# A gated linear recurrence with a feed-forward layer on one core: the fourth pair of chunks laid out one token per partition, the first states scaled straight from PSUM, and a new written order

## The chip, the cores and the metric

The kernel runs on 1 NeuronCore of one Trainium2 chip. The core has five engines with their own instruction queues: TensorE (PE, matrix products and turns), VectorE (DVE), ScalarE (ACT), GpSimd (POOL) and SyncE (SP, which here issues only DMA). The metric is the device time of one execution in microseconds (us), lower is better. Times come from three runs without a profile and from one execution with a profile.

## The reference

Inputs in float32: q, k, v, f_logit of shape (4 batches, 8 heads, 768 tokens, 48), w_in (384, 2048), w_out (2048, 384). A gated linear recurrence runs along the tokens for each batch and head, its output is laid out as 3072 rows of 384, and a feed-forward layer with SiLU follows:

```python
f = 1.0 / (1.0 + np.exp(-f_logit))
for t in range(S):
    state = f[:, :, t, :, None] * state + np.einsum('bhd,bhe->bhde', k[:, :, t], v[:, :, t])
    y[:, :, t] = np.einsum('bhd,bhde->bhe', q[:, :, t], state)
x = y.transpose(0, 2, 1, 3).reshape(B * S, H * D)
h = x @ w_in
g = h * (1.0 / (1.0 + np.exp(-h)))
out = g @ w_out
```

## The kernel before, in words

**Tiling.** The 768 tokens of a batch are cut into 6 chunks of 128. A chunk of one batch is a unit, and two units make one of 12 pairs (table `PAIRS`, line 19). In a pair of form 'T' both units are consecutive chunks of one batch, and a partition holds two consecutive tokens of all heads; a load then moves pieces of 2 x 48 floats, 384 bytes. In a pair of form 'N' a partition holds one token of each unit, and a piece is 48 floats, 192 bytes. Pairs 0 to 3 are T and take the chunks 0 and 1 of the batches 0 to 3; the pairs 4 to 11 are N and take the same chunk of two batches.

**Steps of a unit**, by the names of the written order, with the line of their code:
- `f`, `q`, `k`, `v`: loads, on SP's queue (239). `wi`, `wo`: the weights in 4 pieces each, on POOL's queue (216, 219).
- `E`, `L`: exponential and logarithm on ACT (246, 258, 261), which give the log of the gate; `cs`: its running sum over the chunk, a product with a triangle on TensorE (322, 326 for T; 329, 332 for N); `ia`, `a`, `al`: exponentials of that sum on ACT (334, 276, 336).
- `ki`, `qg`: k and q times these factors, on VectorE or POOL (339). `vb`: v as bfloat16 (187 or 185: the two lines of the copy helper).
- `tq`: turn of both by TensorE (346), and `qkc`: the copy out of PSUM; or `qkD`: the turn by one DMA on SP's queue (354). The pairs 0 to 3 and a few later units use `tq`.
- `sc`: scores (363 for T, 367 for N); `at`: masking on VectorE (371).
- `y`, `yi`: products with the values and with the state (283, 379, 383); `d`: the chunk's own addition to the state (295 for T, 400 for N); `sd`: its sum with the state before, or for a first chunk a plain copy (404, 187 or 185); `su`: that times `al`, two pieces of 48 partitions, which gives the next state (414, on POOL).
- `yc`: y as bfloat16; then `yT` and `xc`, turn on TensorE (391) and copy; or `yD`, turn by DMA (395). This gives xT of the pair.
- `mi.P.j`: two of the 16 column blocks of x @ w_in for the 256 tokens of pair P (269); the pairs 0 and 1 do it in two halves of 128 tokens. `si.P.j`: SiLU on ACT (274). `mo.P.i.n`: a quarter of the sum over the 16 blocks for the output of unit i (304). `oc`, `so`: copy out of PSUM and store.

**Order.** Every engine goes through its steps in the order in which they stand in the string `PLAN` (line 37); a word is the step, the engine (P TensorE, A ACT, V VectorE, G POOL, S SP) and the number of the buffer that the result takes. A step that waits holds back all that stands behind it on its engine, and this goes for SP's loads and turns too. `idle.512.n` are n products without use, of 512 columns, which fill time on TensorE. PSUM has 8 buffers (`pb`), q, k and v have 6 each, f has 4. ACT changes its table of functions where the order goes from exponentials to SiLU or back (475, 507).

`su` reads `sd` where the order has such a step, and otherwise `d` in PSUM (408); both ways were in the code already:

```python
if ("sd", P, i) in names:
    src = at("sd", P, i)
else:
    src = at("d", P, i)[:, 0:HD].rearrange("p (n w) -> p n w", w=2 * D)
```

Of the kernel before, what the change touches and what calls it, by code (L numbers as in the profile page):

```python
# [22 lines left out]
    ('T', (3, 0), (3, 1)),  # L23
# [14 lines left out]
f.0.0:S:0 f.0.1:S: f.2.0:S:1 f.1.0:S:2 q.0.0:S:0 E.0.0:A:0 E.0.1:A: k.0.0:S:0 L.0.0:A:0 L.0.1:A: idle.512.11::0 cs.0.1:P:0 E.2.0:A:1 k.1.0:S:1  # L38
cs.0.0:P:1 ia.0.1:A:0 v.0.0:S:0 E.1.0:A:0 ia.0.0:A:1 q.1.0:S:1 a.0.0:A:2 L.1.0:A:1 qg.0.0:G:0 L.2.0:A:2 f.3.0:S:3 idle.512.5::2 cs.1.1:P:2 ki.0.0:V:
al.0:A:0 a.0.1:A:3 ki.0.1:V:1 cs.1.0:P:3 ia.1.1:A:4 cs.2.0:P:4 k.2.0:S:2 qg.0.1:V: ia.1.0:A:2 tq.0.0:P:5 ki.1.1:V:2 a.1.0:A:1 cs.2.1:P:6 ki.1.0:V:3  # L40
a.1.1:A:0 q.2.0:S:2 tq.0.1:P:7 vb.0.0:A:0 vb.0.1:V:1 ia.2.1:A:3 qkc.0.1:V:0 d.0:P:1,0 qkc.0.0:A: qg.1.0:V: v.1.0:S:1 qg.1.1:V: sd.0.0:A:0
idle.512.3::3 sc.0.0:P:3,7 al.2:A:1 ia.2.0:A:4 su.0.0:G:0 sc.0.1:P:5,1 f.4.0:S:0 at.0.0.1:V:0 E.3.0:A:0 at.0.0.0:V: tq.1.0:P:7 al.1:A:2 a.2.0:A:2
wi.1:G: v.2.0:S:2 at.0.1.0:V:1 tq.1.1:P:2 L.3.0:A:0 qkc.1.1:V:1 qkc.1.0:A: ki.2.1:G:4 idle.512.1::3 cs.3.1:P:3 at.0.1.1:V: cs.3.0:P:4 a.3.1:A:1
ki.2.0:V:0 wi.0:G: sc.1.0:P:5,2 ia.3.1:A:0 at.1.0.0:V:2 y.0:P:7,1 a.2.1:A:3 qg.2.0:G: al.3:A:3 yc.0.0:A:0 at.1.0.1:V: q.3.0:S:3 sc.1.1:P:6,3
vb.1.1:A:2 yi.0.1:P: qg.2.1:G: at.1.1.1:V:3 yT.0.0:P:5 vb.1.0:A:3 tq.2.0:P:7 yc.0.1:A:1 at.1.1.0:V: d.1:P:2,3 a.3.0:A:4 wi.2:G: yT.0.1:P:1 sd.1.0:A:1
tq.2.1:P:6 xc.0.1:V:0 ia.3.0:A:2 xc.0.0:V: su.1.0:G:0 k.3.0:S:3 y.1:P:2,1 qkc.2.0:A:0 sd.0.1:V:0 mi.0.3.0:P:4 yc.1.0:V:2 mi.0.3.1:P: wi.3:G:
qkc.2.1:V: yi.1.1:P: mi.0.2.0:P:5 yc.1.1:A:0 yT.1.0:P:0 su.0.1:G:0 mi.0.2.1:P: xc.1.0:V:1 E.4.0:A:1 yT.1.1:P:7 xc.1.1:V: sc.2.1:P:2,6 sd.1.1:V:1
sc.2.0:P:1,0 L.4.0:A:1 mi.1.2.1:P:7 at.2.1.0:V:0 mi.1.3.1:P:3 mi.1.3.0:P: at.2.0.0:V:1 k.4.0:S:4 mi.1.1.0:P:2 at.2.1.1:V: mi.1.1.1:P: mi.1.2.0:P:
at.2.0.1:V: si.0.2:A:0 mi.0.1.0:P:1 mi.0.1.1:P: si.1.1:A:1 mi.1.0.0:P:6 si.1.2:A: mi.0.0.1:P:5 vb.2.1:G:4 mi.1.0.1:P: vb.2.0:A:5 wo.0:G: mi.0.0.0:P:
# [24 lines left out]
xc.5.1:A: ki.8.1:V:1 q.8.1:S: yc.6.1:A:0 cs.7.0:P:5 vb.8.0:V:4 a.8.0:A:4 mi.5.0:P:1 yc.6.0:V:2 a.7.0:A:1 yD.6.1:S:2 oc.4.0:V:3 al.8.0:A:5 cs.7.1:P:6
# [35 lines left out]
def kernel(  # L110
# [10 lines left out]
    nc = tc.nc  # L121
    B, H, S, D = q.shape
# [57 lines left out]
    at = lambda *key: where[key]  # L180
# [360 lines left out]
```

## Time and profile before

| | us |
|---|---|
| Median of three runs (lowest to highest) | 186.18 (183.22 to 188.34) |
| The profiled execution | 181.74 |
| Its span, first to last instruction | 179.9 |
| TensorE busy in the span | 170.3 (95%) |
| ACT, VectorE, POOL busy | 134.9, 83.2, 59.9 |
| Packets of SP's DMA queue | 69.1% of 16 engines' span |
| Packets of POOL's DMA queue | 16.0% |

The span lies 1.84 us under the profiled execution's time; the profiled execution is 1.48 us under the lowest of the three runs and 4.44 us under their median. Each answer of the trace gives start and length in us from the span's first instruction. "L304" is line 304 of the kernel. In the view of stretches, each line has the stretch, its length, the busy time of PE, PE's weight loads, DVE, ACT and POOL, then the granted TensorE clock (1.00 is full), the DMA share and GB/s. In the view of waits a line is: who waited for whom, us in total, times, the longest. Steps in the text are named as in the written order, for example `y.7.1` for unit 1 of pair 7.

### The profile page before, as it was taken

What the parts mean: (1) busy time and instruction counts of PE and PEld (TensorE: products, weight loads), DVE (VectorE), ACT (ScalarE), POOL (GpSimd) and SP (SyncE); (2) the same over time, 40 slices, a digit from 0 to 9 for tenths busy, and PEclk for the clock granted to TensorE, in tenths of its full rate; (3) what the DMA queues carried; (4) which work ended last, traced back from release to release, by engine and by line L of the source; (5) the groups of instructions that cost most, each with busy time, mean ns of one, the idle gap of its engine ahead of it and who ended that gap; (6) DMA issues with size and microseconds to landing.
All of it is one profiled execution on the core that took longest, in us unless ns stands there. A gap on an engine that the chain in (4) does not pass through costs nothing.

```text
span 179.9 us, 4982 instructions
## 1 busy us (share of the span) xinstructions
PE 170.3 (95%) x2039; PEld 130.0 (72%) x2040; DVE 83.2 (46%) x165; ACT 134.9 (75%) x252; POOL 59.9 (33%) x107
## 2 busy tenths in 40 slices
PE   6978599999999999999999999998999999999992
PEld 2355589998666787679688877787866877887782
DVE  7089977343710263793666064551058758000010
ACT  4899759999936899887997969783896971278321
POOL 6027753695200370140464500581305220003030
PEclk9999879999999999999999999999999999999999
DMA  5999999999989997999949999698985951314043
GB/s 142 315 321 309 202 242 256 230 209 193 180 176 182 203 201 134 210 204 207 158 106 221 178 202 205 125 218 170 216 156 122 213 127 26 109 26 131 0 154 112
DMA packets 109574, 31.91 MB, mean 177 GB/s; under 512 B 103536, under 2 KB 109088, under 8 KB 109552
## 3 DMA queue, kind: packets, MB, share of 16 engines
q1 hardware_dynamic: 104928, 26.19, 69.1%
q0 software_dynamic: 4624, 5.41, 16.0%
q8 instruction: 16, 0.26, 0.6%
q14 instruction: 6, 0.05, 0.1%
HBM read 25.17 MB, written 4.72 MB: 166 GB/s over the span
## 4 chain that ended last, share of the span: by engine, by line
PE 84%; ACT 6%; DVE 3%; DMA 2%; issue 2%; POOL 0%; POOLq 0%; DVEq 0%
PE pb L304 33%; PE pb L269 33%; PE pb L459 3%; DMA xT<-yb 2%; ACT x L334 2%; PE pb L346 2%; PE pb L379 2%; PE pb L383 2%; PE pb L367 2%; DVE atm L371 2%; PE pb L329 2%; DVE qk L339 1%; PE pb L391 1%; PE pb L295 1%; PE pb L363 1%
## 5 line engine op out<-in xcount | busy, mean ns | idle before, releaser
L304 PE MATMUL pb<-w_out_sb,hT 128*128 128x384 bf16 (+1 forms) x416 | 70.7, 313 | 0.1
L269 PE MATMUL pb<-xT,w_in_sb 128*128 128x256 bf16 (+1 forms) x672 | 70.1, 257 | 0.7 <-DMA xT<-yb 0.5
L274 ACT ACTIVATE hT<-pb 128x512 bf16<-128x512 f32 x96 | 51.0, 611 | 23.2 <-PE pb L269 23.1
L269 PEld LDWEIGHTS <-w_in_sb 128*128 128x128 bf16 x672 | 56.9, 98 | 8.2 <-issue 0.9
L304 PEld LDWEIGHTS <-hT 128*128 128x128 bf16 x416 | 37.9, 97 | 18.1
L414 POOL TENSOR_TENSOR st<-sd,al 48x192 bf16<-48x192 f32 x40 | 20.6, 516 | 54.7 <-PE pb L379 18.2
L371 DVE TENSOR_TENSOR atm<-pb,triu 128x512 bf16<-128x512 f32 x32 | 20.0, 682 | 15.2 <-PE pb L367 15.2
L187 DVE COPY ob<-pb 128x384 f32<-128x384 f32 (+1 forms) x16 | 8.3, 526 | 36.0 <-PE pb L304 35.9
L334 ACT ACTIVATE x<-pb 128x384 f32<-128x384 f32 x48 | 22.0, 511 | 3.3 <-PE pb L329 1.5
L507 ACT ACT_TABLE_LOAD x17 | 21.8, 1283 | 0.3
L339 POOL TENSOR_TENSOR qk<-k,x 128x384 bf16<-128x384 f32 x11 | 11.4, 1038 | 14.9 <-DVE vb L187 13.5
L339 DVE TENSOR_TENSOR qk<-k,x 128x384 bf16<-128x384 f32 x13 | 11.9, 936 | 8.3 <-DMA k<-in_k_dram 5.4
L404 DVE TENSOR_TENSOR sd<-pb,st 128x384 f32<-128x384 f32 x16 | 8.6, 550 | 12.6 <-PE pb L400 6.1
L316 POOL DMA_DIRECT2D out_dram<-ob x7 | 4.0, 569 | 29.5 <-ACT ob L185 21.1
L339 DVE TENSOR_TENSOR qk<-q,x 128x384 bf16<-128x384 f32 x17 | 11.4, 688 | 3.3 <-DMA q<-in_q_dram 1.8
L246 ACT ACTIVATE e<-f 128x768 f32<-128x768 f32 (+1 forms) x13 | 10.5, 804 | 2.0 <-DMA f<-in_f_logit_dram 2.0
L185 ACT CAST yb<-pb 128x384 bf16<-128x384 f32 x16 | 7.6, 490 | 3.6 <-PE pb L383 2.4
L371 DVE TENSOR_TENSOR atm<-pb,mask 128x512 bf16<-128x512 f32 x16 | 10.1, 680 | 0.4 <-PE pb L363 0.4
L339 POOL TENSOR_TENSOR qk<-q,x 128x384 bf16<-128x384 f32 x7 | 7.1, 1019 | 7.4 <-ACT x L334 5.8
L459 PE MATMUL pb<-zero,triu 128*128 128x512 bf16 x19 | 7.1, 525 | 1.5 <-POOL triu masks.py:66 1.4
L185 ACT COPY ob<-pb 128x384 f32<-128x384 f32 (+1 forms) x10 | 4.4, 456 | 4.6 <-PE pb L304 4.6
L346 PE MATMUL pb<-ident,qk 128*128 128x128 bf16 x80 | 6.7, 234 | 0.4 <-DVE atm L371 0.4
(72 smaller groups left out, 153.2 us busy)
## 6 DMA issues: line engine op xcount, KB each, us to landing
f<-in_f_logit_dram SPq DMA_DIRECT2D x11, 384.0 KB, 5.5
k<-in_k_dram SPq DMA_DIRECT2D x16, 192.0 KB, 3.7
v<-in_v_dram SPq DMA_DIRECT2D x16, 192.0 KB, 4.3
q<-in_q_dram SPq DMA_DIRECT2D x16, 192.0 KB, 4.2
q<-in_q_dram SPq DMA_DIRECT2D x4, 384.0 KB, 5.2
k<-in_k_dram SPq DMA_DIRECT2D x4, 384.0 KB, 4.9
v<-in_v_dram SPq DMA_DIRECT2D x4, 384.0 KB, 7.3
w_in_sb<-in_moe_w_in_dram POOLq DMA_DIRECT2D x4, 384.0 KB, 7.5
```

Of the source, the lines that this page charges most:

```text
L185: nc.scalar.copy(dst, src)
L246: return nc.scalar.activation(e, at("f", P)[:, j * w:(j + 1) * w], AF.Exp, scale=-1.0)
L269: nc.tensor.matmul(h[:, i, cols], w_in_sb[:, kk, n * 128:(n + 1) * 128], at("xT", P)[:, kk, cols], start=(kk == 0), stop=(kk == KT - 1))
L274: return nc.scalar.activation(at("hT", P)[:, 2 * j:2 * j + 2, :], at("h", P, j).rearrange("p (n c) -> p n c", n=2), AF.Silu)
L304: nc.tensor.matmul(at("o", P, i)[:, cols], at("hT", P)[:, n, i * C:(i + 1) * C], w_out_sb[:, n, cols], start=(n == 0), stop=(n == NT - 1))
L334: nc.scalar.activation(at(kind, P, i).rearrange("p h d -> p (h d)"), at("cs", P, i)[:, 0:HD], AF.Exp, scale=1.0 if kind == "ia" else -1.0)
L339: ENG[eng].tensor_mul(at("qk", P, i)[:, j, :, 0:D], heads("qk"[j], P, i), at("ia" if j else "a", P, i))
L346: nc.tensor.transpose(t_ps[:, j, p, :], at("qk", P, i)[:, j, 2 * p:2 * p + 2, :], ident)
L371: ENG[eng].tensor_mul(at("atm", P, i)[:, r], at(f"s{r}", P, i).rearrange("p (n c) -> p n c", c=C), mask[:, None, :].to_broadcast([C, NP, C]))
L414: ENG[eng].tensor_mul(at("st", P, i)[lo:lo + D, :, r * D:(r + 1) * D], src[lo:lo + D, :, r * D:(r + 1) * D], al_of(P, i)[lo:lo + D, :, Non ...
L459: nc.tensor.matmul(buf["pb", int(got)][:, 0:rest[0]], triu, zero[:, 0:rest[0]], start=True, stop=True, skip_group_check=True)
L507: nc.scalar.preload_act_table_set(TABLES[mode])
```

## The change

Three things change.

1. Pair 3 is of form N instead of T: its two units are still the chunks 0 and 1 of batch 3, but a partition holds one token of each. Its loads have 192-byte pieces and are cut in two, each half the chunk of one unit. Since the load's address used to assume that the units of an N pair differ in the batch, one line is added that takes batch and chunk of the half's own unit. Pair 3's q and k are turned by TensorE (`tq.3.0`, `tq.3.1`), as before.
2. The steps `sd.0.0`, `sd.1.0`, `sd.2.0` and `sd.3.0` are gone from the order: `su` of these first chunks reads the products `d` in PSUM and runs on VectorE instead of POOL.
3. The whole written order is another one, with other engines and buffers for many steps. The dummy products are 27 instead of 20, in 6 places instead of 4.

A form of `qkD` for T pairs is added to the code and not used by the order.

```diff
@@ PAIRS
     ('T', (2, 0), (2, 1)),
-    ('T', (3, 0), (3, 1)),
+    ('N', (3, 0), (3, 1)),
     ('N', (0, 2), (1, 2)),
@@ PLAN, the beginning
-f.0.0:S:0 f.0.1:S: f.2.0:S:1 f.1.0:S:2 q.0.0:S:0 E.0.0:A:0 E.0.1:A: k.0.0:S:0 L.0.0:A:0 L.0.1:A: idle.512.11::0 cs.0.1:P:0 E.2.0:A:1 k.1.0:S:1
+f.0.1:S:0 f.0.0:S: f.3.0:S:1 q.0.0:S:0 f.1.0:S:2 E.0.1:A:0 k.0.0:S:0 E.0.0:A: L.0.1:A:0 L.0.0:A: v.0.0:S:0 idle.512.10::0 cs.0.0:P:0 cs.0.1:P:1
+a.0.0:A:0 k.1.0:S:1 ia.0.0:A:1 E.3.0:A:1 a.0.1:A:2 q.1.0:S:1 al.0:A:0 E.1.0:A:0 qg.0.1:V:0 qg.0.0:V:1 ia.0.1:A:3 f.2.0:S:3 ki.0.0:G: L.1.0:A:1
+ki.0.1:V: idle.512.6::2 cs.1.1:P:2 vb.0.1:A:0 f.3.1:S: vb.0.0:V:1 L.3.0:A:2 tq.0.1:P:3 ia.1.1:A:4 cs.1.0:P:4 v.1.0:S:1 ki.1.1:G:2 tq.0.0:P:5 a.1.0:A:2
+a.1.1:A:0 d.0:P:6,7 ia.1.0:A:1 qg.1.1:V: k.2.0:S:2 su.0.0:V:0 qg.1.0:G:3 idle.512.3::0 tq.1.1:P:0 q.2.0:S:2 qkc.0.1:V:0 E.2.0:A:0 cs.3.0:P:1 wi.0:G:
+sd.0.1:V:0 qkc.1.1:A:1 v.2.0:S:2 qkc.0.0:V: wi.1:G: L.2.0:A:0 idle.512.5::4 sc.0.0:P:4,6 ki.1.0:V: q.5.0:S:3 at.0.0.0:V:0 vb.1.1:G:2 idle.512.1::3
+tq.1.0:P:3 vb.1.0:G:3 at.0.0.1:V: qkc.1.0:A: sc.0.1:P:7,5 at.0.1.0:V:1 cs.2.1:P:0 al.3.0:A:1 cs.2.0:P:4 k.6.1:S:3 at.0.1.1:V: al.1:A:2 ia.2.1:A:3
...
@@ PLAN, around f.7.0 and the xT of pair 4
+mo.2.0.3:P: si.3.3:A: si.3.4:A: sc.4.1:P:3,5 sc.4.0:P:1,7 oc.1.0:A:4 at.4.1.0:V:0 v.7.1:S:4 d.5.1:P:6 d.5.0:P:4 mi.3.2:P:2 at.4.1.1:V: qkD.5.0:S:0
+sd.5.0:V:0 d.4.0:P:3 si.3.2:A: mo.3.0.0:P:5 qg.5.1:V: y.4.1:P:4 at.4.0.0:V:1 mo.3.0.1:P: yc.4.1:A:0 su.4.1:G:0 at.4.0.1:V: mo.3.1.0:P:2 oc.2.0:V:5
+cs.6.0:P:1 ki.6.1:V: qkD.5.1:S:1 mo.3.0.2:P: E.7.0:A:0 sd.4.0:V:1 y.4.0:P:4 mo.3.1.1:P: L.7.0:A:1 vb.7.1:V:5 q.7.0:S:1 su.4.0:G:0 yT.4.1:P:7
+mo.3.1.2:P: xc.4.1:A:0 v.6.1:S: yc.4.0:A:1 cs.7.0:P:0 sd.5.1:V:1 cs.7.1:P:3 yT.4.0:P:7 q.7.1:S: ia.7.1:A:1 mo.3.1.3:P: al.7.0:A:4 a.7.0:A:2
+mo.3.0.3:P: xc.4.0:A: oc.3.1:V:2 qkD.6.1:S:2 ia.6.0:A:4 mi.4.7:P:4 oc.3.0:V:1 ia.7.0:A:0 ki.6.0:G:0 al.7.1:A:5 a.7.1:A:3 mi.4.3:P:6 ki.7.1:V:4
...
@@ emit, loads of an N pair
                 n = 2 // parts
                 w = n * HD
+                if n == 1:
+                    b, c = us[j][0] - j, us[j][1]
                 src = SRC[kind].rearrange("b h s d -> s (b h) d")[c * C:(c + 1) * C, (b + j * n) * H:(b + (j + 1) * n) * H]
@@ emit, qkD
-            nc.sync.dma_start_transpose(out=at("qkT", P, i).rearrange("p j n c -> p (j n) c"), in_=at("qk", P, i).rearrange("p j h d -> p (j h d)"))
+            if T:
+                dst = at("qkT", P).rearrange("p j n g s c -> p (j n) g s c")[:, :, :, i]
+            else:
+                dst = at("qkT", P, i).rearrange("p j n c -> p (j n) c")
+            nc.sync.dma_start_transpose(out=dst, in_=at("qk", P, i).rearrange("p j h d -> p (j h d)"))
```

125 lines of the change are left out of this document (58 added, 67 removed).

## The prediction

> **What bounds the kernel now.** The page's head, its busy shares and its DMA slices are read first. What matters is that TensorE is nearly full and that the 16 DMA engines are close to full for two thirds of the span.
>
> ```profile
> span 179.9 us, 4982 instructions
> PE 170.3 (95%) x2039; PEld 130.0 (72%) x2040; DVE 83.2 (46%) x165; ACT 134.9 (75%) x252; POOL 59.9 (33%) x107
> ...
> DMA  5999999999989997999949999698985951314043
> ```
>
> The first `mi` step (first product with w_in) starts at 25.17 us by the timeline of TensorE. The last `mo` ends at 176.77: there the chain that ended last goes over to ACT's copy of ob.
>
> ```profile
> 25.17 0.84 PE L269 MATMUL pb<-xT,w_in_sb 128*128 128x128 bf16 x12
> ```
>
> ```profile
> 176.77 0.32 ACT ob L185
> ```
>
> The view of busy time by stretch, cut at these two points, shows where TensorE is empty.
>
> ```profile
> 0.00:25.17 25.17, 19.50 (x285) 12.33 (x287) 17.43 (x47) 19.55 (x41) 11.04 (x29) 0.93 1.06 259
> 25.17:176.77 151.60, 150.78 (x1760) 117.64 (x1754) 65.73 (x119) 115.09 (x212) 48.90 (x79) 1.00 0.84 166
> 176.77:179.90 3.13, 0.00 (x0) 0.00 (x0) 0.00 (x0) 0.31 (x1) 0.00 (x0) 1.00 0.26 84
> ```
>
> The middle stretch has 0.82 us of idle in 151.60. So nothing can be won there but work, and much can be lost: any wait that is put in front of TensorE lengthens the span one for one. The start (25.17 us) is where time can be won. The third view, the waits of TensorE, agrees: the only wait of more than 1.5 us is for the masking `at` on VectorE, in the start, and the only one for a transfer is 0.5 us.
>
> ```profile
> PE pb L391 <- DVE atm L371: 1.7, 1, 1.7
> PE pb L322 <- ACT lf L258: 1.5, 2, 1.2
> ...
> PE pb L269 <- DMA xT<-yb: 0.5, 1, 0.5
> ```
>
> So there are three sums: when the first `mi` starts, how much work stands behind it, and whether a load in the new order comes after TensorE wants it.
>
> **1. The start.** The first fence is VectorE's timeline, the second the timeline of all engines, the third the groups of instructions with shapes kept apart (busy us, mean ns).
>
> ```profile
> 11.04 0.56 DVE L339 TENSOR_TENSOR qk<-q,x 128x384 bf16<-128x384 f32 x1
> ...
> 12.73 0.68 DVE L187 COPY qkTT<-pb 128x1024 bf16<-128x1024 bf16 x1
> ...
> 17.86 3.02 DVE L339 TENSOR_TENSOR qk<-k,x 128x384 bf16<-128x384 f32 x1
> 20.80 2.47 DVE L371 TENSOR_TENSOR atm<-pb,mask 128x512 bf16<-128x512 f32 x4
> ...
> 24.70 0.55 DVE L404 TENSOR_TENSOR sd<-pb,st 128x384 f32<-128x384 f32 x1
> ```
>
> ```profile
> 18.48 1.97 POOL L339 TENSOR_TENSOR qk<-q,x 128x384 bf16<-128x384 f32 x2
> ```
>
> ```profile
> L414 POOL TENSOR_TENSOR st<-sd,al 48x192 bf16<-48x192 f32 x40 | 20.6, 516 | 54.7 <-PE pb L379 18.2 <-DVE sd L404 10.9 <-DVE qk L339 9.1
> ...
> L185 ACT COPY sd<-pb 128x384 f32<-128x384 f32 x3 | 1.5, 512 | 2.2 <-PE pb L295 2.2
> ...
> L187 DVE COPY ob<-pb 128x192 f32<-128x192 f32 x2 | 0.7, 358 | 21.4 <-PE pb L304 21.4
> ```
>
> Before, `ki.2.0` of the third pair stands on VectorE between the eight masking steps of pairs 0 and 1. It takes 3.02 us, all through the two POOL multiplications that run from 18.48 to 20.45, where the like step at 11.04 takes 0.56. The last mask ends at 20.80 + 2.47 = 23.27, `y.1` follows, and `mi` comes 1.9 us after that mask.
>
> After, VectorE's order from `qg.1.1` on is: `qg.1.1`, `su.0.0`, `qkc.0.1`, `sd.0.1`, `qkc.0.0`, `ki.1.0`, eight masks; nothing of pair 2 stands among them. `su.0.0` is new on VectorE: two pieces of 192 columns read from PSUM. No row shows this operation there; the nearest is the 192-column copy from PSUM at 358 ns, so 0.7 us (bounds: 0.4 us as it has 48 partitions and not 128, if that helped; 1.1 us if it went like the 550 ns of 384 columns). In exchange an ACT copy (0.51) and two POOL pieces (1.03) leave the way from `d.0` to the state, and the pairs 1 and 2 save the same; there VectorE has the cover of its 46%. At `su.3.0` the masks `at.3.1` stand behind it, and `y.3.1`, which waits for them, has some 2.6 us of other TensorE steps ahead; without that cover it would cost 0.7.
>
> The sum: 0.56 + 0.7 + 0.68 + 0.55 + 0.68 + 0.56 + 8 x 0.62 (2.47 / 4) = 8.7 us. It starts when q of pair 1 is in. DMA begins at about 2 us and goes at this rate (a GB/s line of the DMA view for 2 to 14 us):
>
> ```profile
> GB/s 183 262 266 274 280 169 230 306 320 323 302 323 325 324 324 324 326 301 291 306 323 317 305 321 325 324 327 325 326 321 325 323 328 316 310 306 328 320 301 303
> ```
>
> A 384 KB load (0.393 MB) at 320 GB/s is 1.23 us. Up to `q.1.0` the new order has seven of them and one half of `f.3` at 1.05 (worked out in part 3): 2.0 + 8.6 + 1.05 = 11.7, and some 0.5 to the waiting instruction, 12.2. The last mask ends at 20.9, and with the 1.9 us behind it the first `mi` would start at 22.8. To that I add 0.7 us for POOL: `ki.0.0`, `ki.1.1` and `qg.1.0` now run on POOL beside multiplications on VectorE. The bounds are 0 and three POOL pieces of 1.0 us each, 3.0; 0.7 is near the low end since only `qg.1.1` against `qg.1.0` falls on the chain. **First `mi` at 23.5, a gain of 1.7** (2.4 to -0.6).
>
> The Trainium skill, SBUF — State Buffer, section "SBUF: two separate sides", says that VectorE and GpSimd share a port pair under an exclusive lock, which a VectorE operation with two inputs in SBUF and a GpSimd operation hold for their whole length. The 3.02 us row agrees; taken for all three places it makes the upper bound of 3.0 and a rival below.
>
> The dummy products (`idle`) grow from 20 to 27. They stand in waits: `idle.512.6` ends near 9, and `cs.1.1` behind it waits for `L.1.0`, which ended at 10.5 before and has f of pair 1 about a microsecond later now; `idle.512.5` ends some 0.5 before `qkc.0.0`, by the VectorE sum. Without that cover each product costs about 0.22 (estimate: 512 columns by the 384-column products of part 2, 1.32 / 8).
>
> ```profile
> 8.98 1.58 ACT L258 ACTIVATE lf<-e 128x768 bf16<-128x768 f32 x2
> ```
>
> **2. The work behind the first `mi`.** Rows of the chain that ended last, start, us, step:
>
> ```profile
> 41.19 0.45 PE pb L346 x8
> ...
> 45.34 0.45 PE pb L295 x16
> 45.79 0.57 PE pb L363 x32
> ...
> 50.37 0.51 PE pb L283 x32
> ...
> 54.24 0.17 PE pb L379 x4
> 54.66 1.32 PE pb L304 x8
> ...
> 60.74 0.65 PE pb L269 x6
> ...
> 70.18 0.19 PE pb L400 x4
> ...
> 71.67 0.55 PE pb L367 x16
> ...
> 75.10 0.20 PE pb L383 x8
> ```
>
> A step of `mo` or of whole `mi` is 0.65, a turn `tq` 0.45. Pair 3 as N: products with the values 2 x 0.20 + 0.17 for 0.51 + 0.17, `d` 2 x 0.19 for 0.45, scores 0.55 for 0.57: 0.2 us less. Behind the first `mi` come the two turns `tq.2` (+0.90), which stood in front of it; `yi.1.1` and `yT.1.0` go in front (-0.34). Sum **+0.4**. The `mi` and `mo` counts are the same.
>
> **3. The loads.** Pair 3 changes from 384-byte to 192-byte pieces.
>
> ```profile
> DMA packets 9721, 1.86 MB, mean 186 GB/s; under 512 B 9720, under 2 KB 9720, under 8 KB 9720
> ```
>
> This is the stretch 50 to 60 us, in which nearly all is 192-byte loads: 0.197 MB at 186 GB/s is 1.05 us per half pair, 2.1 a pair against 1.23. Pair 3 has four arrays: 3.5 us more of DMA time early, in a stretch where the engines are full. TensorE does not wait for pair 3 itself (`q.3.0`, `k.3.0` come some 5 us ahead), but all later loads move.
>
> The tightest I find is `f.7.0`. Before, `q.5.0` is issued at 58.24 and takes 3.7 us, so lands at 61.9:
>
> ```profile
> 58.24 0.76 SPq L239 DMA_DIRECT2D q<-in_q_dram  x1
> ```
>
> ```profile
> DMA to landing us min/median/max: 3.7/3.7/3.7
> ```
>
> Up to there 16 large loads, 22 halves and all 8 weight pieces had gone. After, up to `f.7.0`, it is 12 large, 36 halves, the same weights, one turn of qk by DMA (0.26 MB, 1.4 us at the same rate) and an output: 61.9 - 4 x 1.23 + 14 x 1.05 + 1.4 + 0.6 = 73.7; at the 0.99 us that a half takes where the engines are never idle it is 72.9. I take 73.3. Behind it on ACT stand, in this order, with the means of these rows (page and groups):
>
> ```profile
> L334 ACT ACTIVATE x<-pb 128x384 f32<-128x384 f32 x48 | 22.0, 511 | 3.3 <-PE pb L329 1.5 <-PE pb L332 1.1 <-PE pb L326 0.4
> ...
> L246 ACT ACTIVATE e<-f 128x768 f32<-128x768 f32 x11 | 9.4, 855 | 0.4 <-DMA f<-in_f_logit_dram 0.3
> L261 ACT ACTIVATE lf<-e 128x768 bf16<-128x768 f32 x8 | 6.8, 849 | 0.2
> ...
> L185 ACT COPY xT<-pb 128x384 bf16<-128x384 bf16 x4 | 1.9, 481 | 1.9 <-PE pb L391 1.8
> ```
>
> `E.7`, `L.7` (1.7), then `xc.4.1` and `yc.4.0` (0.5 each), two exponentials and a small one (1.0, from 511 ns each less the overlap of their ends), `xc.4.0` (0.5). So the first whole `mi.4` can't start before 73.3 + 4.2 = 77.5. TensorE's own line: from the first `mi` to there, 32 half and 16 whole `mi` 21.2, 32 `mo` 20.8, the rest 10.8, together 52.8. Priced so, the middle stretch of before is 149.2 where it took 151.6, so 53.7: 23.5 + 53.7 = 77.2. **A wait of 0.3.** Before, `f.7.0` had about 10 us in hand at its `cs.7.0`.
>
> The later loads (`f.10`, `f.9`, `k.8.1`) come out 0 to 4 us ahead; `mi.8` starts 3.9 us of steps after `y.8.1`, which is what yb needs through a DMA turn. I cost them at nothing; a turn that meets a full queue costs 1 to 3.
>
> **Sum**: -1.7 + 0.4 + 0.3 = -1.0; span 178.9. The profiled execution is 181.74, 1.84 around its span, so 180.7. The median of the runs shown is 186.18, 4.4 above that execution, and I cannot see in one profile what the others lost; the forecast keeps that distance: 186.18 - 1.0 = **185.2**.
>
> **The rivals.**
>
> *The load queue takes over (slower).* Place: `f.7.0` and the ACT steps behind it. For: the DMA slices; three runs that spread over 5 us. Against: TensorE waits only 0.5 us for transfers before. All the gain is gone when `f.7.0` lands at 74.3, and from 78.0 the kernel is over 2% slower (3.7 us). With a landing 5 us late (7%) it is -1.0 + 5.0 = +4.0: 190.2. Chance 0.25.
>
> *Late transfers hurt less (faster).* The 4.4 us of the unprofiled runs would go. Before has a place with nothing in hand, `mi.7`, which waits for its turned yb:
>
> ```profile
> 119.08 4.43 DMA xT<-yb
> ```
>
> There the new order has `yD.7.1` some 2 us ahead. Against it stands the smaller lead at `f.7`. If 3.5 to 4 of the 4.4 us go: 181.4. Chance 0.22.
>
> *The start isn't shortened.* VectorE is held by POOL at three places, first `mi` at 25.9: +0.7 + 0.4, no wait at `f.7`: 187.3. Chance 0.13.
>
> The forecast, 185.2, has 0.40.
>
> **How the numbers follow.** A measurement of this kernel tells 2%, 3.7 us, from no change. Faster by more: 0.22 and a little of the forecast's tail, 0.24. Slower by more: 0.25 and a little of the others, 0.28. Within: 0.48. Range 181.0 to 190.2: it reaches both outer rivals' times and leaves out about 2 in 10. The likeliest case alone is 183.5 to 187.
>
> **What the new profile would show.** First `mi` near 23.5 and no VectorE multiplication of 3 us between masks (step 1); a middle stretch of about 152.3 us with `mi` and `mo` counts unchanged (step 2); `f.7.0` landing near 73 and TensorE waiting under 1 us around 76, for lf or for xT from `xc.4.0` (step 3). I am wrong if TensorE waits several us for lf, qkT or xT between 60 and 120, if the start is no shorter, or if the spread of runs goes.

## The result, and the profile after

The kernel changed takes 188.12 us (median of four runs, 185.94 to 188.39), the kernel before beside it 184.95 (183.22 to 188.34). The ratio is **1.025, with a 95% interval of 1.020 to 1.030**: slower. Ratios in this document compare only the executions within 1.5% of a kernel's fastest, while the times are medians of all its executions, so the two need not agree (the ratio of experiment 2 rests on three of ten executions, that of 7 on six of ten). The forecast was 185.2, a gain of 1.0 on the forecast's own base. The profiled execution took 187.98 us with a span of 186.0, which is 6.1 us more span than in the profile of before.

The page of the kernel changed, its head, busy times and DMA slices:

```profile
span 186.0 us, 4923 instructions
...
PE 173.0 (93%) x2003; PEld 131.0 (70%) x2005; DVE 78.3 (42%) x167; ACT 131.5 (71%) x251; POOL 61.0 (33%) x102
...
DMA  5999999999989999999999999899286766021015
GB/s 122 287 308 227 194 245 176 185 178 191 224 167 176 198 182 237 208 186 165 241 247 191 193 178 191 124 177 271 50 167 154 166 151 155 3 46 42 0 63 190
```

TensorE is busy for 2.7 us longer (173.0 for 170.3) and empty for 3.4 us longer (13.0 for 9.6). In the start it is busy for 1.1 us less (18.38 for 19.50), though seven dummy products came in there; behind the first `mi` it is busy for 3.9 us more (154.6 for 150.8). Part of that is the clock, below, and part is work that the forecast did not have (step 2, further down). The DMA engines are as busy as before, but from the third to the eighth slice (9 to 37 us) they move less on the whole: 308, 227, 194, 245, 176, 185 GB/s, where before had 321, 309, 202, 242, 256, 230 (slices of 4.65 and 4.5 us).

Busy time by stretch of the kernel changed (first `mi`, end of the start, `mi.5.1`, last product):

```profile
0.00:23.60 23.60, 18.38 (x281) 10.72 (x284) 14.70 (x47) 16.78 (x37) 10.78 (x28) 1.00 0.98 228
23.60:34.00 10.40, 8.53 (x118) 8.11 (x115) 3.68 (x8) 6.71 (x14) 4.39 (x6) 0.84 1.18 206
34.00:97.00 63.00, 61.46 (x773) 47.12 (x770) 32.41 (x60) 49.84 (x94) 26.43 (x40) 1.00 1.06 200
97.00:182.90 85.90, 84.65 (x838) 65.09 (x838) 27.54 (x52) 57.83 (x108) 19.37 (x29) 1.00 0.62 133
```

The start became shorter, as forecast: the first `mi` is at 23.60 and no longer at 25.17. But the stretch behind it, which was full before (0.82 us of idle in 151.60), now has 1.9 us of idle in its first 10.4 us, at a mean granted clock of 0.84, and then 1.5 and 1.3 us more, most of which is one wait of 1.78 us at `mi.5.1` that the cut at 97.00 divides. TensorE's timeline shows the places (start, us, step, in brackets the wait ahead of it):

```profile
23.60 0.93 PE L272 MATMUL pb<-xT,w_in_sb 128*128 128x128 bf16 x12
25.78 0.51 PE L272 MATMUL pb<-xT,w_in_sb 128*128 128x128 bf16 x6 [1.25 <-DMA w_in_sb<-in_moe_w_in_dram]
...
27.08 3.36 PE L272 MATMUL pb<-xT,w_in_sb 128*128 128x128 bf16 x30 [0.62 <-DVE xT L188]
...
97.44 1.48 PE L272 MATMUL pb<-xT,w_in_sb 128*128 128x256 bf16 x12 [1.78 <-DMA xT<-yb]
...
178.42 2.79 PE L307 MATMUL pb<-w_out_sb,hT 128*128 128x192 bf16 x28 [0.41 <-ACT ob L186]
```

`mi.0.3.1` waits 1.25 us for the second piece of w_in. Then comes a wait of 0.62 for xT, `xc.0.0` on VectorE. VectorE's timeline says why `xc.0.0` is late: it stands behind `qg.2.1`, and that multiplication waited 2.77 us for q of pair 2.

```profile
22.32 0.72 DVE L421 TENSOR_TENSOR st<-pb,al 48x192 bf16<-48x192 f32 x2 [0.24 <-PE pb L298]
...
26.20 0.56 DVE L342 TENSOR_TENSOR qk<-q,x 128x384 bf16<-128x384 f32 x1 [2.77 <-DMA q<-in_q_dram]
26.68 0.35 DVE L188 COPY xT<-pb 128x384 bf16<-128x384 bf16 x1
```

And behind these two waits the granted clock falls to a half. The view of busy time, microsecond by microsecond (the number behind the busy times is the clock):

```profile
27.00:28.00 1.00, 0.92 (x10) 0.92 (x10) 1.00 (x4) 0.98 (x3) 1.00 (x2) 0.55 1.16 192
28.00:29.00 1.00, 1.00 (x12) 1.00 (x11) 0.23 (x1) 1.00 (x1) 0.01 (x1) 0.50 1.00 174
29.00:30.00 1.00, 1.00 (x12) 1.00 (x11) 0.00 (x0) 0.05 (x1) 0.00 (x0) 0.50 1.14 185
30.00:31.00 1.00, 1.00 (x17) 1.00 (x15) 0.00 (x0) 0.00 (x0) 0.00 (x0) 0.74 1.18 172
```

So the 30 products at 27.08 took 3.36 us; experiment 5 below has the same 30 at full clock in 1.90. That is 1.5 us more of lost time, and it is counted as busy.

The kernel before has such a stretch too, but inside its start, at the wait of 1.7 us for the masks. The same view of the kernel before, one of the three microseconds from 21 to 24, all at 0.50:

```profile
22.00:23.00 1.00, 1.00 (x15) 0.80 (x14) 1.00 (x3) 0.00 (x0) 0.00 (x0) 0.50 1.23 220
```

So the half clock is not new. It went out of the start, whose mean is now 1.00 for 0.93, and came back behind the first `mi`.

### The profile page after: what moved, and what is told of

Read it like the earlier page. It is cut to its first block, busy times and chain, and to the rows that moved or that the text cites. A ratio compares the mean times of both kernels' runs of the same rounds, so it can differ in the third digit from the quotient of the medians.

```text
span 186.0 us, 4923 instructions
## 1 busy us (share of the span) xinstructions
PE 173.0 (93%) x2003; PEld 131.0 (70%) x2005; DVE 78.3 (42%) x167; ACT 131.5 (71%) x251; POOL 61.0 (33%) x102
## 3 DMA queue, kind: packets, MB, share of 16 engines
HBM read 25.17 MB, written 4.72 MB: 161 GB/s over the span
## 4 chain that ended last, share of the span: by engine, by line
PE 70%; DMA 13%; SPq 7%; ACT 6%; issue 2%; DVE 1%; DVEq 0%; ACTq 0%
PE pb L272 32%; PE pb L307 28%; SPq L242 7%; DMA q<-in_q_dram 6%; DMA xT<-yb 3%; DMA f<-in_f_logit_dram 3%; PE pb L374 2%; ACT L514 2%; PE pb L349 1%; PE pb L390 1%; PE pb L386 1%; ACT hT L277 1%; ACT ob L186 1%; PE pb L332 1%; PE pb L407 1%
## 5 line engine op out<-in xcount | busy, mean ns | idle before, releaser
L272 PE MATMUL pb<-xT,w_in_sb 128*128 128x256 bf16 (+1 forms) x672 | 71.7, 261 | 3.9 <-DMA xT<-yb 1.8
L378 DVE TENSOR_TENSOR atm<-pb,triu 128x512 bf16<-128x512 f32 x36 | 23.1, 685 | 36.6 <-PE pb L374 25.2
L342 POOL TENSOR_TENSOR qk<-k,x 128x384 bf16<-128x384 f32 x12 | 12.7, 1055 | 36.7 <-ACT x L337 15.3
L421 POOL TENSOR_TENSOR st<-sd,al 48x192 bf16<-48x192 f32 x32 | 16.9, 528 | 19.5 <-PE pb L386 12.5
L342 POOL TENSOR_TENSOR qk<-q,x 128x384 bf16<-128x384 f32 x11 | 11.8, 1074 | 30.3 <-DMA q<-in_q_dram 12.1
L514 ACT ACT_TABLE_LOAD x15 | 19.2, 1283 | 0.3
L188 DVE COPY ob<-pb 128x384 f32<-128x384 f32 (+1 forms) x12 | 6.2, 522 | 21.5 <-PE pb L307 20.3
L342 DVE TENSOR_TENSOR qk<-q,x 128x384 bf16<-128x384 f32 x13 | 7.5, 584 | 11.2 <-ACT x L337 8.4
L186 ACT COPY ob<-pb 128x384 f32<-128x384 f32 (+1 forms) x14 | 6.5, 466 | 6.7 <-PE pb L307 6.7
L342 DVE TENSOR_TENSOR qk<-k,x 128x384 bf16<-128x384 f32 x12 | 8.1, 675 | 5.9 <-ACT x L337 3.5
L264 ACT ACTIVATE lf<-e 128x768 bf16<-128x768 f32 (+1 forms) x10 | 7.8, 788 | 0.1
L378 DVE TENSOR_TENSOR atm<-pb,mask 128x512 bf16<-128x512 f32 x12 | 7.4, 684 | 0.1
```

The lines of the kernel that those rows point to most:

```text
L186: nc.scalar.copy(dst, src)
L272: nc.tensor.matmul(h[:, i, cols], w_in_sb[:, kk, n * 128:(n + 1) * 128], at("xT", P)[:, kk, cols], start=(kk == 0), stop=(kk == KT - 1))
L342: ENG[eng].tensor_mul(at("qk", P, i)[:, j, :, 0:D], heads("qk"[j], P, i), at("ia" if j else "a", P, i))
L378: ENG[eng].tensor_mul(at("atm", P, i)[:, r], at(f"s{r}", P, i).rearrange("p (n c) -> p n c", c=C), mask[:, None, :].to_broadcast([C, NP, C]))
L421: ENG[eng].tensor_mul(at("st", P, i)[lo:lo + D, :, r * D:(r + 1) * D], src[lo:lo + D, :, r * D:(r + 1) * D], al_of(P, i)[lo:lo + D, :, Non ...
L514: nc.scalar.preload_act_table_set(TABLES[mode])
```

## The experiments

Two theories stood after this reading. **The pieces**: pair 3's loads of 192 bytes slow the loads of the first 40 us, the things that have no lead there (q of pair 2, w_in) come late, and the rest follows. **The order**: the new order puts single steps at bad places (`qg.2.1` ahead of `xc.0.0`, w_in pieces behind a POOL multiplication, `f.11.0` ahead of a turned yb, the last output products), whatever the loads are. The first states on VectorE were a third part to be cleared. Ratios below are to the kernel before on the same chip, with 95% intervals.

**1. Pair 3 as N alone**, in the order of before, halves side by side.

```diff
-('T', (3, 0), (3, 1))
+('N', (3, 0), (3, 1))
-f.3.0:S:3
+f.3.0:S:3 f.3.1:S:
-v.3.0:S:3
+v.3.0:S:3 v.3.1:S:
...
-d.3:P:5,0
+d.3.0:P:5 d.3.1:P:0
```

> The order of before, with pair 3 alone laid out one token per partition (its loads in halves of 192-byte pieces, its value products and states per unit). Theory 'order' (the loss lies in single places of the new order, not in the layout): within 1 us of before, since TensorE has 0.2 us less work and no load of pair 3 was late before. Rival 'layout' (pair 3's smaller pieces make the whole DMA queue late): 2 to 3.5 us slower than before, with waits of TensorE behind loads of the pairs 4 to 7.

Measured: 187.04 us, ratio 1.025 (1.015 to 1.035): a loss of the same size is there without the new order. The waits of TensorE in this kernel, and POOL's timeline:

```profile
PE pb L402 <- POOL vb L187: 3.3, 1, 3.3
...
PE pb L297 <- ACT vb L185: 2.1, 3, 1.3
```

```profile
32.48 0.50 POOL L187 CAST vb<-v 128x384 bf16<-128x384 f32 x1 [6.32 <-DMA v<-in_v_dram]
...
47.46 0.50 POOL L187 CAST vb<-v 128x384 bf16<-128x384 f32 x1 [8.47 <-DMA v<-in_v_dram]
```

In the old order v is what comes late: v of pair 2 holds `d.2`, and v of pair 3 holds POOL for 8.47 us and `d.3.0` on TensorE for 3.3. By the packet records v of pair 2 has landed at 32.0 where before has it at 24.5, and v of pair 3 at 45.2 instead of 37.3.

**2. First states from PSUM alone**, in the order of before.

```diff
-sd.0.0:A:0
-su.0.0:G:0
+su.0.0:V:0
...
-sd.3.0:V:0
-su.3.0:G:0
+su.3.0:V:0
```

> The order of before, with the copies sd of the four first chunks left out and su reading PSUM on VectorE. Theory 'order': 0 to 1 us faster or no change; su costs VectorE 0.72 us each, measured in the changed kernel. Rival 'first states' (VectorE's masks are pushed back by su and the first products with them): 1 to 3 us slower than before, first mi 0.7 us or more later.

Measured: 184.22 us, ratio 0.999 (0.993 to 1.006). No effect either way can be told. The median of all executions is 0.8% above the 182.75 of the kernel before, so a small cost is not excluded. The loss of 2.5% does not come from here: experiment 1 has it without this part, and experiment 5 has this part without the loss.

**3. Two moves in the start** of the kernel changed: `qg.2.1` behind `xc.0.0` on VectorE, the first two w_in pieces ahead of `qg.1.0` on POOL.

```diff
+wi.0:G:
+wi.1:G:
 qg.1.0:G:3
...
-wi.0:G:
...
-wi.1:G:
...
-qg.2.1:V:
...
 xc.0.0:V:
+qg.2.1:V:
```

> The changed kernel with two moves: VectorE's multiplications of q of pair 2 behind the copy xc.0.0, and the first two weight pieces ahead of qg.1.0 on POOL. Theory 'order': the 0.6 us wait for xT goes, the 1.25 us wait for the weights shrinks to about 0 to 0.3, and the half clock from 27.3 to 30.5 us, which costs 1.5 us, goes with them: span 186.0 - 2 to - 3.5, so 182.5 to 184. If the clock falls all the same: 184.5 to 185. Rival 'layout': the loads arrive as late as before, 186 within 0.7.

Measured: 185.49 us, ratio 1.017 (1.006 to 1.028). The w_in wait is gone, and another has come: `yT.1.1` now waits for ACT's `ia` to free a PSUM buffer. TensorE's timeline of this kernel:

```profile
26.20 0.33 PE L398 MATMUL pb<-ident,yb 128*128 128x128 bf16 x3 [1.01 <-ACT x L337]
26.36 1.89 PE L272 MATMUL pb<-xT,w_in_sb 128*128 128x128 bf16 x30
```

The 30 products took 1.89 us here: no half clock behind this wait. Later, at `mi.5.1`, this profile has a wait of 1.84 us for the turned yb. The interval overlaps that of the kernel changed, so the gain of these moves by themselves is not settled by this run.

**4. `f.11.0` behind the turned yb** `yD.6.1`, in the kernel changed.

```diff
-f.11.0:S:2
...
 yD.5.0:S:1
...
 yD.6.1:S:2
+f.11.0:S:2
```

> The changed kernel with one load, f.11.0, moved behind the two turns of yb of the pairs 5 and 6 on SP's queue. Theory 'order': the wait of 1.8 us in front of mi.5.1 goes, span 184.1 (183.8 to 184.5). Rival 'layout' (the whole queue is late, one load more or less in front changes little): 185.5 to 186.3, with the wait kept or moved to the next turned yb.

Measured: 187.29 us, ratio 1.024 (1.015 to 1.034): no gain that can be seen. Its trace is of an execution of 347 us, so whether the wait was there is left open by this run.

**5. The kernel changed with wide pieces.** Pair 3's loads go by the 384-byte form: the same number of bytes to the same places of SBUF, but of other tokens, so pair 3's result isn't the reference's. Nothing else is changed.

```diff
-            if T:
+            if T or P == 3:
                 h = H // parts
```

> The changed kernel, with pair 3's loads taking the 384-byte pieces of form T (the same bytes into the same places of the buffers, but other tokens; all else as in the change, so pair 3's numbers are those of other tokens, which leaves the work as it is). Theory 'pieces' (192-byte pieces queued next to the weights make every load behind them late): the second weight piece and q of pair 2 land 1.5 to 5 us earlier, the first mi block loses its waits and its half clock; 2 to 4 us faster than the changed kernel, 1.00 to 1.01 of before. Theory 'order': less than 1 us faster than the changed kernel, since its waits come from single places of the order.

Measured: 182.82 us, ratio 1.000 (0.998 to 1.003). The whole loss is gone with the piece size, but the gain of 1.0 us that was forecast is not there either (step 2, further down, says why). TensorE's timeline, to be held against the rows of the kernel changed:

```profile
23.00 0.93 PE L272 MATMUL pb<-xT,w_in_sb 128*128 128x128 bf16 x12
24.45 0.51 PE L272 MATMUL pb<-xT,w_in_sb 128*128 128x128 bf16 x6 [0.52 <-DMA w_in_sb<-in_moe_w_in_dram]
...
24.97 1.90 PE L272 MATMUL pb<-xT,w_in_sb 128*128 128x128 bf16 x30
```

The first `mi` is 0.6 us earlier, the w_in wait 0.52 and no longer 1.25, the wait for xT and the half clock are gone, and there is no wait at `mi.5.1`. The next fences are the view by stretch, 14 to 20 us (last number GB/s), and the row for q of pair 2 in the view of DMA issues from 14 to 40 us (last number: us from issue to landing). First the kernel changed:

```profile
14.00:20.00 6.00, 5.25 (x104) 3.28 (x106) 5.87 (x12) 4.55 (x10) 3.58 (x5) 1.00 1.02 212
```

```profile
q<-in_q_dram SPq DMA_DIRECT2D x1, 384.0 KB, 11.2
```

and the same with wide pieces:

```profile
14.00:20.00 6.00, 5.03 (x101) 2.97 (x100) 5.89 (x11) 5.16 (x11) 3.33 (x5) 1.00 1.20 280
```

```profile
q<-in_q_dram SPq DMA_DIRECT2D x1, 384.0 KB, 6.0
```

The packet records show how a small delay grows. The second half of f of pair 3 has landed at 15.5 with small pieces and at 14.1 with wide ones, 1.4 us; k of pair 2 at 20.1 against 16.5, 3.6 us; q of pair 2 at 24.1 against 19.2, 4.9 us. In both kernels the first packets of w_in, on POOL's queue, come at 17.4. With wide pieces k of pair 2 is through by then (1.2 us from its first to its last packet) and q of pair 2 takes 2.7; with small ones k meets them and takes 3.5 us, and q behind it 4.1. The Trainium skill, DMA: Bandwidth & Descriptors, section "Queues, rings and completion order", says that each DMA engine goes round its queues packet by packet. The trace agrees as far as it goes: the same load of k took 1.2 us without w_in packets beside it and 3.5 us with them. The 11.2 us against 6.0 of q, in the rows above, hold the wait behind k as well.

**6. Experiment 1 with wide pieces** (same edit as in 5, pair 3's result again of other tokens).

> The order of before with pair 3 laid out one token per partition, as in the run with pair 3 alone, but with 384-byte pieces in its loads (other tokens, the same work). Theory 'pieces': the 4.3 us that the layout cost come back, 1.00 of before within 0.5%, v of pair 3 lands at 37 to 38 us and not at 45. If it is the work or the waits of the N form and not the pieces: still 1.02.

Measured: 183.97 us, ratio 1.003 (0.999 to 1.006). Of the 2.5% of experiment 1, 0.3% is left, and that is not told from nothing. The piece size is the cause of the loss in both orders.

**7. All moves in the kernel changed**: those of 3 and 4, and the second half columns of `mo.11.0` behind `mo.11.1.3.0`, so that the last copies have time.

```diff
-mo.11.0.0.1:P:
 oc.11.0.0:A:2
-mo.11.0.1.1:P:
...
-mo.11.0.2.1:P:
...
 mo.11.1.3.0:P:
-mo.11.0.3.1:P:
 oc.11.1.0:V:3
 so.9.1:S:
+mo.11.0.0.1:P: mo.11.0.1.1:P: mo.11.0.2.1:P: mo.11.0.3.1:P:
 mo.11.1.0.1:P:
```

> The changed kernel with four local moves together: the two of the start, f.11.0 behind the turned yb, and the first halves of the last products interleaved so that no product waits for a copy out of the same PSUM buffer. Theory 'order': -1.5 (start, as measured), -1.8 (mi.5.1), -0.8 (tail) = 4.1 us faster than the changed kernel, span 182. Theory 'pieces': the start's part stays and the wait at mi.5.1 comes back at the next load: 2 to 2.5 us faster, span 183.5 to 184.

**8. The kernel changed once more**, beside 7.

> The changed kernel itself once more, on the chip of the other runs of this call, to compare them with it: 1.025 of before, and the waits at the same places: 1.2 us for the weights, 0.6 for xT in the first mi block, half clock there, 1.8 before mi.5.1.

Measured: 184.77 us, ratio 1.006 (1.003 to 1.010) for all moves; 186.88 us, 1.022 (1.016 to 1.029) for the kernel changed again. So the moves give back 1.6% of the time, with the small pieces in place. The second profile of the kernel changed has the wait for w_in, longer, and the half clock behind it, but no wait at `mi.5.1`; in its timeline:

```profile
26.75 0.81 PE L272 MATMUL pb<-xT,w_in_sb 128*128 128x128 bf16 x6 [1.82 <-DMA w_in_sb<-in_moe_w_in_dram]
...
27.67 3.05 PE L272 MATMUL pb<-xT,w_in_sb 128*128 128x128 bf16 x30
```

q of pair 2 has landed at 22.4 here by the packet records, 1.7 us earlier than in the first profile, and no wait for xT is left: what both profiles have late is the w_in piece. The wait at `mi.5.1` comes in the first profile (1.78) and in that of experiment 3 (1.84), and not here; it varies between executions, and the start's loss is there in both profiles of this kernel.

**9 to 11. Pair 3 back in form T in the new order.** Here the pieces are 384 bytes and the whole reference is computed; products and state steps of pair 3 stay apart by half as the order has them. 9 has the moves of 7 but leaves `qg.2.1` where it is, 10 has them all. In 11 the w_in pieces stay at their places, and `wo.1`, `wo.2` stand ahead of `qg.3.1` on POOL (the last part of the diff).

```diff
-('N', (3, 0), (3, 1))
+('T', (3, 0), (3, 1))
-cs.3.0:P:1
...
+cs.3.0:P:1
 cs.3.1:P:5
...
-al.3.0:A:1
...
-al.3.1:A:4
+al.3:A:4
...
-qkc.3.0:A:0
+qkc.3.0:A:1
...
-qkc.3.1:A:1
+qkc.3.1:A:
...
+vb.3.1:V:2
 at.3.0.1:V:2
...
 at.3.0.0:V:
+at.3.1.1:V:3 at.3.1.0:V:
...
-at.3.1.1:V:3
...
-at.3.1.0:V:
...
-vb.3.1:V:2
...
 y.3.1:P:6
+yi.3.1:P:
...
-                    for r in range(2):
+                    for r in rest[1:] or (0, 1):
...
-            todo = [r for r in range(2) if us[r][1] < CHUNKS - 1]
+            todo = [r for r in rest[1:] or (0, 1) if us[r][1] < CHUNKS - 1]
...
-            return [(kind, P, i) for i in range(2) if kind == "y" or PAIRS[P][1 + i][1] < CHUNKS - 1]
+            return [(kind, P, i) for i in rest[1:] or (0, 1) if kind == "y" or PAIRS[P][1 + i][1] < CHUNKS - 1]
```

```diff
+wo.1:G: wo.2:G:
 qg.3.1:G:
...
-wo.1:G:
...
-wo.2:G:
```

> The new order with pair 3 back in form T (two tokens per partition, pieces of 384 bytes, the whole reference is computed; its products with the values and its state steps stay apart by half as the order has them), and with three of the four moves: the first two weight pieces ahead on the load-issuing order of POOL, f.11.0 behind the turned yb, the last output products in another order. Theory (the small pieces cost the 4 us, and the moved places are worth their own waits on top): the order with wide pieces stood at 1.000 of the kernel before and the moves were worth 1.6% on the small pieces, so 0.984 to 0.99, 180 to 181 us where the kernel before takes 183; the first mi near 23, no wait at mi.5.1 and none at the tail. Rival (with wide pieces nothing is late any more, so the moves have only the tail of 0.85 us and the weight wait of 0.8 us left to win): 0.991 to 0.995. Second rival (the new order itself is worse than the one before, and only the other tokens of the wide-piece run hid it): 1.00 or more.

> As the run beside it, and qg.2.1 behind xc.0.0 on VectorE as well. Theory: with wide pieces q.2 comes about 1 us earlier than the small pieces let it, and the move puts its turn later, so it wins no more than 0.3 us and may bring the 0.5 to 0.7 us wait of yT.1.1 for PSUM that the run with all moves showed: within 0.5% of the run beside it. Rival (qg.2.1 is what starts the half-clock stretch whatever the pieces): 1 to 1.5 us less than the run beside it, 0.976 to 0.982 of the kernel before.

> The new order with pair 3 in form T (the whole reference is computed), f.11.0 behind the turned yb and the last output products in another order, as in the two runs before; but the weight pieces of w_in stay at their places, and the pieces wo.1 and wo.2 stand ahead of qg.3.1 on POOL. In form T qg.3.1 waits for both halves of q.3 (the run before shows POOL held 12.6 us there, and TensorE 2.1 us late for w_out behind it). Theory (form T lost its gain to that wait and to the w_in pieces that made q.2 late): first mi near 23.0, no wait for w_out, its form T has 1.1 us more of products than form N; 0.995 to 1.003 of the kernel before. Rival (two consecutive tokens in this order are late at every step of pair 3 and after it): 1.01 to 1.02, with waits at mo.1 and tq.3 as in the run before.

Measured: 187.74 us, 1.017 (1.010 to 1.025); 188.49 us, 1.017 (1.009 to 1.026); 189.48 us, 1.032 (1.028 to 1.037). The theories of 9 and 11 fell, and 11 came out worse than its rival's 1.01 to 1.02 as well. That of 10 held as far as it went: the further move changed nothing that can be told. The second rival of 9, that the new order itself is worse and the other tokens of experiment 5 hid it, forecast 1.00 or more, and there the ratios lie; no run here excludes it. The traces show another cause for part of the loss. POOL's timeline of 9 and TensorE's waits:

```profile
40.99 0.99 POOL L341 TENSOR_TENSOR qk<-q,x 128x384 bf16<-128x384 f32 x1 [12.60 <-DMA q<-in_q_dram]
```

```profile
PE pb L306 <- DMA w_out_sb<-in_moe_w_out_dram: 2.1, 2, 1.1
```

In form N a unit needs its own half of q, k and v; in form T each unit needs both halves. So `qg.3.1` holds POOL 12.60 us for the other half, and the w_out pieces behind it come late. With wide pieces in form N (experiment 12) the same step waits half as long:

```profile
33.54 0.99 POOL L341 TENSOR_TENSOR qk<-q,x 128x384 bf16<-128x384 f32 x1 [6.01 <-DMA q<-in_q_dram]
```

In 11, where they stand ahead of it, the same thing holds ACT: `vb.3.0` waits for the second half of v, and the SiLU steps behind it keep TensorE for 2.2 us. ACT's timeline and TensorE's waits of 11:

```profile
47.84 0.51 ACT L185 CAST vb<-v 128x384 bf16<-128x384 f32 x1 [2.29 <-DMA v<-in_v_dram]
```

```profile
PE pb L306 <- ACT hT L276: 2.2, 1, 2.2
```

The first `mi` is at 24.09 in 11, and at 23.00 in 5. The running sum of pair 3, which form T needs whole right there, takes 0.9 us; the half of it that stands there in form N takes 0.3 in 5 (19.89 to 20.22). So 0.6 of the 1.1 us is the running sum (TensorE's timeline of 11, ahead of `y.0`):

```profile
20.48 0.32 PE L324 MATMUL pb<-lf,tincl 128*128 128x384 bf16 x1
20.64 0.32 PE L324 MATMUL pb<-lf,tstrict 128*128 128x384 bf16 x1
20.81 0.49 PE L324 MATMUL pb<-lf,tincl 128*128 128x384 bf16 x2
21.13 0.34 PE L328 MATMUL pb<-halves,lf 128*128 128x2 bf16 x8
21.40 0.57 PE L285 MATMUL pb<-vb,atm 64*128 64x48 bf16 x32
```

In 9 the two waits for w_out (2.1) and the later start (23.98 for 23.11) make 3.0 of the 6.2 us of span that it has over 12; the rest is not followed. My reading, not shown by a run of its own, is that the new order is written for units that come one by one, and only form N, with its small pieces, gives it that.

**12. All moves and wide pieces**, the fourth corner beside the kernel changed, 5 and 7 (pair 3's tokens as in 5).

> The kernel changed with all moves (w_in pieces ahead, qg.2.1 behind xc.0.0, f.11.0 behind the turned yb, the last output products in another order) and pair 3's loads in pieces of 384 bytes, which are the same bytes of other tokens, so that pair 3's result isn't the reference's; its work is unchanged. The fourth corner beside the order as it is (1.022), with all moves (1.006) and with wide pieces alone (1.000). Theory (the moves and the wide pieces win the same time twice: the early waits; only the tail and the turned yb are the moves' own): 0.993 to 0.997. Rival (they add up): 0.984. Second rival (with the w_in pieces ahead, q.2 comes late whatever the pieces of pair 3): 1.00 to 1.01, first mi near 23.7 and not 23.0, and a wait at tq.2.1 or yT.1.1.

Measured: 182.54 us, ratio 0.999 (0.996 to 1.002), nearest to the first theory and a little short of it. The moves are worth 1.6% with small pieces and 0.2%, which is nothing that can be told, with wide ones. So they won no time of their own that can be told: they moved the steps out of the way of late loads, and where the loads aren't late there is little to win. In its profile the first `mi` is at 23.11, there is no wait for w_in and none in the tail, yet the span (180.1) is only 0.7 under that of 5: some time comes back at later places, which are not followed here.

No kernel here computes the reference in less time than the kernel before.

## Why the prediction was wrong, step by step

**The base.** The forecast kept 4.4 us between the profiled execution of before and the median of three runs. In the later comparisons the kernel before had medians of 182.7 to 183.5 (11 to 25 runs), 1.0 to 1.8 us above that execution. The distance of 4.4 was chance. The measured loss stands by the ratio, not by this.

**Step 1, the start: right in the number, partly by luck.** Forecast 23.5, measured 23.60. VectorE's steps from `qg.1.1` to the last mask took 8.5 us where 8.7 were summed (13.55 to 22.08), and the two pieces of `su`, priced at 0.7 us, took 0.72 (row above). No multiplication stands among the eight masks, and none of VectorE's steps there took longer than summed:

```profile
17.17 4.91 DVE L378 TENSOR_TENSOR atm<-pb,mask 128x512 bf16<-128x512 f32 x8
```

So the rival "the start isn't shortened" fell, and the 0.7 us added for POOL were not needed. But the sum began at 12.2, and VectorE could begin only at 13.55: q of pair 1 landed at 13.5, 5.2 us after its issue. And from the last mask to the first `mi` it was 1.5 us and not 1.9, since at that place the kernel before ran at half clock (row above) and the kernel changed did not. The late beginning, the unneeded 0.7 and the clock, which no step names, cancel.

**Step 2, the work behind the first `mi`: too small.** It was summed at +0.4 us. In experiment 5, which has the same products at full clock, TensorE is busy for 152.79 us from the first `mi` to the last product, where the kernel before has 150.78: **+2.0**. Experiment 12 has 152.70. The first line is of the kernel changed, with the half clock in it, the second of experiment 5:

```profile
23.60:182.90 159.30, 154.63 (x1726) 120.32 (x1723) 63.63 (x120) 114.39 (x215) 50.19 (x75) 0.99 0.83 164
...
23.00:177.69 154.69, 152.79 (x1726) 118.52 (x1723) 65.18 (x120) 114.42 (x215) 50.35 (x75) 1.00 0.84 166
```

The two turns `tq.2` are 0.9 of the 2.0, as summed; where the rest comes from is not followed. This is why no gain shows even with the loads on time: in the profile of 5 the start is 2.2 us shorter, the work 2.0 longer and the waits behind the first `mi` 1.1 longer, 0.9 us more span than before. In the kernel changed it is -1.6 for the start, +3.9 for the work, half clock included, and +3.9 for waits (4.7 for 0.8): the 6.1 us.

**Step 3, the loads: wrong, and here the sign was lost.** The size was not the main fault: "3.5 us more of DMA time" stands against loads that were 7 to 8 us late in experiment 1 at v of the pairs 2 and 3, and 5.4 at v of pair 4. The step that failed is "The tightest I find is `f.7.0`", behind the right half sentence "but all later loads move". The lead of a load was looked up for pair 3 and for the late loads, but not for the loads that stand between and behind the halves of f of pair 3: q of pair 2 and the w_in pieces. These have no lead in the new order. In step 1 the half of f was priced as one more load of 1.05 us ahead of q of pair 1, and the other half, behind it, not at all. The runs put in the place of a wait of 0.3 us at `f.7.0`: 1.25 us for w_in, 0.62 for xT behind a late q, 1.5 for the half clock behind both, and in one of two profiles of this kernel 1.78 at `mi.5.1`, which the step had costed at nothing and named as "1 to 3" if the queue is full. `f.7.0` itself landed at 76.5 by the packet records, 3.2 later than worked out; ACT waited 0.6 us for it, and TensorE, whose own line was late by then too, lost about 0.2.

**The tail.** The wait of the last products for a copy out of PSUM (0.41, row above) is named in no step; experiment 7 took them away, and 12, without them, isn't measurably faster than 5, with them.

**The rivals.** "The load queue takes over" had the right resource and sign (190.2 forecast, 188.12 measured) and the wrong place: it was put 50 us too late. "Late transfers hurt less" went the other way. So the measured time lay inside the range, and the likeliest case on the wrong side of no change.

**What would have told.** The row for the 192-byte stretch (186 GB/s) and the 7.5 us from issue to landing of the w_in pieces, on the page of before, were both there to be put together: a load at the head of a full queue delays every load behind it, and the first of these without lead sets the price, not the last.

## What to carry to other kernels

When a change makes early transfers slower, list the transfers behind them on the queue in order, and look up the lead of each at its consumer; the price is paid at the first one without lead, and what waits there on an in-order engine (here `qg.2.1` ahead of `xc.0.0`) passes it on. Work that an order moves from the start to behind it is paid for there: with the loads on time the start was 2.2 us shorter here and the work behind it 2.0 longer. A delay is not carried on one for one: 1.4 us at one load became 4.9 us three loads later, because it pushed them under another queue's traffic. Moves that cure such waits look like gains of their own until the loads are on time; test them at both ends before keeping them.

## What the runs showed of the hardware that was not expected

**The clock can fall after waits of under two microseconds.** In the kernel changed waits of 1.25 and 0.62 us, with 0.7 us of work between them, were followed by a granted clock of 0.50; in the second profile a wait of 1.82 was, with the 30 products at 3.05 us, and in the kernel before one of 1.70. By the clock records the half clock lasted 3.41 us each of these times. Behind a single wait of 1.01 (experiment 3) or 0.52 (experiment 5) the same products took 1.89 and 1.90. But the length of the wait does not decide it: behind the 1.78 us at `mi.5.1` in the kernel changed (98 to 101 us) and behind a wait of 2.4 in the start of experiment 8 (11 to 14 us) the clock stayed at 1.00. The Trainium skill, TensorE: Matmul & The Clock Gate, section "What's actually happening", has the half clock come after an idle window of about 3.4 us. The 3.41 us that the half clock lasted agree with such a window, the gaps that brought it on do not: in the cases named TensorE was idle for 1.25 to 1.82 us at once. For this kernel such a wait cost up to 1.5 us more than itself. What of the gaps' length, sum or place decides isn't settled by these runs.

**Wide loads behind small pieces can be slow for a while.** The row of 186 GB/s from which the forecast took its price holds for a stretch of small pieces alone. Here the second half of f of pair 3 has landed at 15.5 us, and from then to the first w_in packet, at 17.4 by the packet records, only 384-byte loads run. The first of the next two lines still holds small pieces in its first half, the second holds none. The view by stretch of the kernel changed (the last two numbers are the busy share of the DMA engines, which comes out over 1 in places, and GB/s):

```profile
15.00:16.00 1.00, 1.00 (x7) 0.29 (x3) 0.97 (x3) 0.92 (x2) 1.00 (x2) 1.00 0.86 229
16.00:17.00 1.00, 0.42 (x17) 0.26 (x16) 1.00 (x3) 1.00 (x2) 0.64 (x1) 1.00 0.98 240
```

and that of experiment 5:

```profile
15.00:16.00 1.00, 0.53 (x3) 0.03 (x1) 1.00 (x3) 1.00 (x2) 1.00 (x2) 1.00 1.17 325
16.00:17.00 1.00, 0.89 (x23) 0.68 (x24) 0.95 (x3) 0.63 (x1) 1.00 (x3) 1.00 1.20 334
```

From 16 to 17 us the same loads move at 240 GB/s instead of 334, with the DMA engines less busy, though no small piece is left in the records. The second profile of the kernel changed (experiment 8) has 301 and 238 in these two stretches, with its last small piece at 15.2, so the slow microsecond is there too, but not right behind the small pieces. Experiment 1, whose small pieces end at 15.3, has 285 from 16 to 17. What slows these loads isn't settled by these runs.
